# PSUM banks as tiles of their own in a fused linear-attention and MLP kernel

## The chip, the cores and the metric

The kernel is one program on one core of one Trainium2 chip. The metric is the time of one execution on the device in microseconds (us), the median of three runs. Five engines work from queues of their own, each in the order in which its instructions stand: TensorE (PE; its weight loads are shown as PEld), VectorE (DVE), ScalarE (ACT), GpSimd (POOL) and SyncE (SP), which issues the transfers here. An instruction can wait for semaphores that other engines raise.

## The reference

Three stages follow each other. Attention without a softmax over scores, for 8 batches, 8 heads, 576 positions and 64 columns a head:

```
q_s = softmax(q, axis=-1);  k_s = softmax(k, axis=2)
x   = einsum(q_s, einsum(k_s, v))          # 4608 tokens x 512
h   = x @ w_in;   g = where(h > 0, h, exp(min(h, 0)) - 1)      # layer 1, 512 -> 2048
x   = g @ w_out                                                # 2048 -> 512
h   = x @ w_in2;  g = (a0 + a1 h + a2 h^2 + a3 h^3) / (1 + |b0||h| + |b1|h^2 + 1e-6)   # layer 2
out = g @ w_out2
```

## The kernel before

Each float32 operand is split into a high and a low part, and a product is made of three matmuls. Tokens are cut into 9 blocks of 512 (index j), the 2048 inner columns into 16 steps of 128 (index f).

*Layer 1* makes, for a block and a step, one PSUM bank of h with 12 matmuls of 512 columns (L913 to L915), which ScalarE reads once (relu, L1075) and VectorE once (elu, L1081). Then 12 matmuls (L952) add into the four `acc` banks. The attention of later batches and the preparation of layer 2's weights run beside it, with their own use of the same banks (L617, L744 and others).

*Layer 2* takes two steps at once: 8 groups (p) for each block, 72 in all, each with 256 inner columns for 512 tokens. h is a 2 x 2 arrangement of pieces of 256 columns and is computed by a scheme with seven products in place of eight. The pieces are A and E in one bank, Bq and C in the next. `product` (L1187) issues six matmuls of 256 columns for each of the seven:

| name | writes | then |
|---|---|---|
| m1 | A | u1: ScalarE copies A to Bq |
| m6 | Bq (adds) | u2: ScalarE copies Bq to SBUF |
| m2, m5 | A, E | |
| m7 | Bq (adds) | u3: ScalarE copies Bq to SBUF |
| | | d1, d2: VectorE, C = E + u3's copy, E = E + u2's copy |
| m4, m3 | Bq, E (add) | h is complete |

The copies are L1196, the two adds L1203. A function of h follows, on both banks at once (128 x 1024): absb, pstart and square read h on ScalarE (L1252, L1262, L1257), pmul and pstep on VectorE (L1282, L1285), qsum on GpSimd (L1265), then root and guess on ScalarE (L1268, L1271), test, newton and pend on VectorE (L1274, L1278, L1289), and the split into high (`hi`, L325) and low part (L328, GpSimd). Eight output steps of three matmuls of 512 columns (L1362) add the result into the `acc` banks; at a block's end ScalarE copies those out and SP stores them. Layer 2's prepared weights come from DRAM in two ring loads for each group (1024 and 768 KB).

The order of the work is made by a planner (`Plan`): it runs a list of operations against assumed durations and records, for each engine, the order; the tile layer is told to keep it and adds the semaphore waits. The order is thus fixed before any wait is known. On ScalarE one group's turn in the steady state reads absb, pstart (of group n-1), u1 (of group n), square (n-1), u2 (n), hi (n-2), u3 (n), root, guess (n-1); on TensorE m1, two or three output steps, m6, m2, perhaps an output step, m5, m7, three output steps, m4, m3, two output steps, with a few variants.

PSUM has eight banks. Four are `acc`. The other four are one tile of four banks, from which `bank` hands out slices by turns:

```
banks = ps_p.tile([P, 4 * TB], F32, tag="ps", name="ps", bufs=1)
...
return warmed(banks[:, i * TB:(i + n) * TB])
```

So layer 1's tiles go round four slices, and layer 2's group n has the slices 0 and 1 or 2 and 3, by turns. Which instruction waits for which is worked out for each tile from the accesses to it.

Of the kernel before, what the change touches and what calls it, by code (L numbers as in the profile page):

```python
# [9 lines left out]
F32 = mybir.dt.float32  # L10
# [3 lines left out]
AF = mybir.ActivationFunctionType  # L14
ALU = mybir.AluOpType
AX = mybir.AxisListType
PSUM = bass.MemoryType.PSUM
DRAM = bass.MemoryType.DRAM

P = 128  # L20
TB = 512
# [173 lines left out]
def linear_attention_elu_rational(  # L195
# [31 lines left out]
    nc = tc.nc  # L227
# [7 lines left out]

    main = ctx.enter_context(tc.tile_pool(name="main", bufs=1))
    acc_p = ctx.enter_context(tc.tile_pool(name="acc_p", bufs=4, space=PSUM))
    ps_p = ctx.enter_context(tc.tile_pool(name="ps_p", bufs=1, space=PSUM))
    dram = ctx.enter_context(tc.tile_pool(name="dram", bufs=1, space=DRAM))
    attn_ctx = ExitStack()  # L240
    at = attn_ctx.enter_context(tc.tile_pool(name="at", bufs=1))
# [21 lines left out]
    op = plan.op  # L263
# [30 lines left out]
    def warmed(ps):  # L294
        for _ in range(plan.spare):
            nc.tensor.matmul(ps[:, 0:P], ident, ident, start=True, stop=True)
        plan.spare = 0
        return ps

    banks = ps_p.tile([P, 4 * TB], F32, tag="ps", name="ps", bufs=1)  # L300
    n_banks = [0]

    def bank(n=1):
        i = n_banks[0] % 4
        n_banks[0] += n
        assert i + n <= 4
        return warmed(banks[:, i * TB:(i + n) * TB])

    def acc_bank():
        return warmed(acc_p.tile([P, TB], F32, tag="acc", name="acc"))  # L310
# [1 line left out]
    def two(ap):  # L312
        return ap.rearrange("p (h c) -> p c h", h=2)
# [191 lines left out]
    pair = {}  # L505
# [645 lines left out]
    def plan_group(j, p):  # L1151
        s = step_of(1, j, 2 * p) - (EARLIER[p] if j == 0 and p < len(EARLIER) else 0)
        b = {}
        w, ((we, wek), (wl, wlk)) = plan_ring(j, p)
        x = xf[j]
# [18 lines left out]
        def u(n):  # L1174
            return b["u"][:, n * HT:(n + 1) * HT]

        def product(region, part, k, form, start):
            def fn(e):
                if k == 0 and part == 0:
                    b["h"] = bank(2)  # L1180
                o = turned(region())
                n = 0
                for i in range(2):
                    for wl_, xl in ((0, 0), (0, 1), (1, 0)):
                        lhsT = w[part][:, k, wl_ * HT + i * P:wl_ * HT + (i + 1) * P]
                        rhs = x["t", form][:, i, xl * HT:(xl + 1) * HT]
                        nc.tensor.matmul(o, lhsT, two(rhs), start=start and n == 0, stop=n == 5, skip_group_check=True)  # L1187
                        n += 1
            return fn

        def copy(dst, src):
            def fn(e):
                if "u" not in b and dst is not Bq:
                    b["u"] = f32_tile(ukind[0], ukind[1], *(ukind[2] if len(ukind) > 2 else []))
                if e == "ACT":
                    nc.scalar.activation(out=dst(), in_=src(), func=AF.Copy)  # L1196
                else:
                    nc.vector.tensor_scalar(out=dst(), in0=src(), scalar1=1.0, scalar2=None, op0=ALU.mult)
            return fn

        def add(dst, ps, n):
            def fn(e):
                nc.vector.tensor_tensor(out=dst(), in0=ps(), in1=u(n), op=ALU.add)  # L1203
            return fn

        def put(name, engines, fn, after, **kw):
# [144 lines left out]
        else:  # L1351
            o = chain(slice(0, 2 * TB), True, keep)
# [14 lines left out]
        for n, (i, q) in enumerate(order):  # L1367
            rank = s + AT["out"] * 2 / PERIOD + n * 0.25
            o = op(PE(0.66), out_mm(i, q), [ready[q], slot_ready[1, 2 * p + q, 1]], rank, follow=[last.get("mm_out")],
                   take=["acc"] if p == 0 and q == 0 else [], free=[(gkind, keep["g"])] if n == 7 else [])  # L1370
# [30 lines left out]
    for n in range(2 * KF):  # L1401
        f, which = divmod(n, 2)
# [10 lines left out]
    for p in range(KF // 2):  # L1413
# [5 lines left out]
        o = op(SP, load, [stored["wo", 2 * p], stored["wo", 2 * p + 1]], step_of(0, NB - 1, 2 * p) + 4.0, take=[f"w{p}_1"], extra=4.5)  # L1419
# [11 lines left out]
    with tc.manual_schedule():  # L1431
# [26 lines left out]
        o = op(SP, load_ab, [in_ops[0, 1, 0]], 0.0)  # L1458
        op(ACT(0.2), minus_a, [o, in_ops[0, 2, 0]], 0.0)
        o = op(ACT(0.2), abs_b1, [o, in_ops[0, 2, 0]], 0.0)  # L1460
# [72 lines left out]
```

## Time and profile before

| | |
|---|---|
| median of 3 runs | 2142.43 us (2139.59 to 2142.44) |
| profiled execution | 2129.99 us, its span 2128.2 us |
| busy in the span | TensorE 1710.3 us (80%), VectorE 1088.3 (51%), ScalarE 1084.9 (51%), GpSimd 686.6 (32%) |
| mean granted TensorE clock | 0.951 |
| DMA | 307.47 MB, 144 GB/s |

The span runs from the first to the last instruction. The granted clock is a share of TensorE's full clock: 1.00 is 2.4 GHz, 0.5 is 1.2 GHz. Layer 2's first product starts at 964.3 us, its last at 2106.6 us. "Idle before, and its releaser" is the time in which an engine stood still before an instruction, and the instruction that ended last among those it waited for.

### The profile page before, as it was taken

Reading aid. Unit: us, or ns where it says so; the run is one execution under the profiler, and the core shown is the slowest. Engines: PE = TensorE matmul, PEld = TensorE weight load, DVE = VectorE, ACT = ScalarE, POOL = GpSimd, SP = SyncE. Lnnn points to the kernel's source line nnn. Section 1 sums busy time; section 2 is a strip of 40 time slices with the busy share of each in tenths; the row PEclk is TensorE's granted clock in tenths of the full one; section 3 lists DMA queues with packets and bytes.
Section 4 is the critical chain, followed back from the end, with each engine's and each line's share of the span. In section 5 each row is a group of like instructions: output and inputs, shape, how many; then the busy total and the mean of one; then the engine's idle time right before and its main releaser. Section 6 shows DMA issues by size and latency. Waiting matters only on the chain.

```text
span 2128.2 us, 25372 instructions
## 1 busy us (share of the span) xinstructions
PE 1710.3 (80%) x9626; PEld 1409.1 (66%) x9626; DVE 1088.3 (51%) x1518; ACT 1084.9 (51%) x1689; POOL 686.6 (32%) x457
## 2 busy tenths in 40 slices
PE   8798878898888898988777777787877777777777
PEld 6576667677677677766656566666656666666666
DVE  7587665656475655212444444444444444444445
ACT  6566554556464554334555545454554545445444
POOL 3002543434353433222353332323333232323322
PEclk9999999999999999999899989999998989999989
DMA  8413542433342421153565444443534444443441
GB/s 311 165 47 117 186 164 89 162 122 127 112 157 92 171 90 75 60 191 131 174 222 180 142 154 154 166 166 143 173 124 158 168 173 145 167 152 107 162 148 35
DMA packets 83338, 307.47 MB, mean 144 GB/s; under 512 B 8720, under 2 KB 8720, under 8 KB 70928
## 3 DMA queue, kind: packets, MB, share of 16 engines
q1 hardware_dynamic: 83216, 305.85, 41.1%
q8 instruction: 76, 1.25, 0.2%
q14 instruction: 46, 0.38, 0.1%
HBM read 238.18 MB, written 67.63 MB: 144 GB/s over the span
## 4 chain that ended last, share of the span: by engine, by line
PE 54%; ACT 20%; DVE 17%; issue 4%; DMA 3%; POOL 1%; SPq 0%; DVEq 0%; ACTq 0%; POOLq 0%
PE ps L1187 20%; PE acc L1362 8%; PE acc L952 8%; PE ps L913 6%; PE ps L915 5%; PE ps L914 5%; DVE p L1285 4%; DVE p L1282 4%; ACT p L1262 4%; ACT s L1257 4%; DVE m L1081 3%; DMA x<-fo 2%; ACT m L1075 2%; ACT m L1196 2%; ACT a L1252 1%
## 5 line engine op out<-in xcount | busy, mean ns | idle before, releaser
L1187 PE MATMUL ps<-xf,ring 128*128 128x256 f32 x3024 | 459.2, 302 | 272.4 <-DVE p L1282 88.8
L1187 PEld LDWEIGHTS ps<-xf,ring 128*128 128x128 f32 x3024 | 404.2, 207 | 368.2 <-DVE p L1282 104.0
L1362 PE MATMUL acc<-w_out,g 128*128 128x512 f32 x1728 | 443.9, 400 | 0.8 <-ACT g L325 0.8
L952 PE MATMUL acc<-gs,w_out 128*128 128x512 f32 x1728 | 411.5, 384 | 7.2 <-DVE gs L328 2.5
L952 PEld LDWEIGHTS acc<-gs,w_out 128*128 128x128 f32 x1728 | 326.8, 191 | 62.2 <-ACT gs L325 4.4
L1265 POOL TENSOR_TENSOR s<-s,a 128x1024 f32<-128x1024 f32 x72 | 168.8, 2345 | 588.2 <-ACT s L1257 577.4
L1362 PEld LDWEIGHTS acc<-w_out,g 128*128 128x128 f32 x1728 | 329.0, 203 | 40.6 <-ACT g L325 1.2
L913 PE MATMUL ps<-xs,w_in 128*128 128x512 f32 x576 | 236.3, 410 | 108.3 <-ACT m L1075 45.9
L1196 ACT ACTIVATE m<-ps 128x256 f32<-128x256 f32 x142 | 54.5, 384 | 357.8 <-PE ps L1187 291.0
L914 PE MATMUL ps<-xs,w_in 128*128 128x512 f32 x576 | 223.8, 389 | 0.0
L328 POOL TENSOR_TENSOR g<-p,g 128x1024 fp32r<-128x1024 f32 (+1 forms) x71 | 167.3, 2356 | 174.4 <-ACT g L325 163.5
L915 PE MATMUL ps<-xs,w_in 128*128 128x512 f32 x576 | 223.4, 388 | 0.0
L913 PEld LDWEIGHTS ps<-xs,w_in 128*128 128x128 f32 x576 | 111.6, 194 | 166.3 <-DVE m L1081 64.4
L1081 DVE SCALAR_TENSOR_TENSOR m<-m,ps 128x512 f32<-128x512 f32 x144 | 98.7, 686 | 237.7 <-PE ps L915 122.9
L1282 DVE TENSOR_TENSOR p<-p,ps 128x1024 f32<-128x1024 f32 (+1 forms) x73 | 88.1, 1206 | 227.8 <-ACT s L1257 111.7
L1075 ACT ACTIVATE m<-ps 128x512 f32<-128x512 f32 x144 | 85.8, 596 | 215.2 <-PE ps L915 130.8
L328 POOL TENSOR_TENSOR gs<-m,gs 128x512 fp32r<-128x512 f32 x85 | 110.0, 1295 | 228.0 <-ACT gs L325 221.5
L1285 DVE SCALAR_TENSOR_TENSOR p<-p,a_sb,ps 128x1024 f32<-128x1024 f32 (+1 forms) x73 | 92.4, 1266 | 142.3 <-PE ps L1187 69.5
L1274 DVE SCALAR_TENSOR_TENSOR s<-s,a 128x1024 f32<-128x1024 f32 (+1 forms) x73 | 89.1, 1222 | 92.2 <-ACT a L1271 90.6
L1203 DVE TENSOR_TENSOR ps<-ps,m 128x256 f32<-128x256 f32 x142 | 61.4, 432 | 145.9 <-ACT m L1196 135.8
L325 ACT ACTIVATE gs<-m 128x512 fp32r<-128x512 f32 x144 | 89.9, 625 | 87.1 <-DVE m L1081 42.7
L1252 ACT ACTIVATE a<-ps,b_sb 128x1024 f32<-128x1024 f32 (+1 forms) x73 | 80.4, 1103 | 87.9 <-PE ps L1187 65.7
(152 smaller groups left out, 2146.8 us busy)
## 6 DMA issues: line engine op xcount, KB each, us to landing
ring<-wf SPq DMA_DIRECT2D x72, 1024.0 KB, 5.2
ring<-wf SPq DMA_DIRECT2D x72, 768.0 KB, 4.6
x<-fo SPq DMA_DIRECT2D x54, 512.0 KB, 2.9
xf<-x SPq DMA_DIRECT2D x47, 512.0 KB, 6.0
wf<-fo SPq DMA_DIRECT2D x24, 512.0 KB, 2.8
out_dram<-e SPq DMA_DIRECT2D x36, 256.0 KB, 2.2
bits<-in_moe_w_in_dram SPq DMA_DIRECT2D x8, 1024.0 KB, 11.2
bits<-in_moe_w_out_dram SPq DMA_DIRECT2D x8, 1024.0 KB, 12.0
```

What stands on the lines that cost most here:

```text
L328: engine[e].tensor_tensor(out=lo, in0=src, in1=hi.bitcast(F32), op=ALU.subtract)
L913: nc.tensor.matmul(o, w[:, 0, kk, :], two(x[:, 0]), start=(kk == 0), stop=False)
L914: nc.tensor.matmul(o, w[:, 0, kk, :], two(x[:, 1]), start=False, stop=False)
L915: nc.tensor.matmul(o, w[:, 1, kk, :], two(x[:, 0]), start=False, stop=(kk == KD - 1))
L952: nc.tensor.matmul(turned(o), lhsT, two(rhs), start=(f == f0 and n == 0), stop=(f == f1 and n == 2))
L1075: nc.scalar.activation(out=b["m"], in_=b["h"], func=AF.Relu, scale=-1.0)
L1081: nc.vector.scalar_tensor_tensor(out=b["m"], in0=b["m"], scalar=-1.0, in1=b["h"], op0=ALU.add, op1=ALU.max)
L1187: nc.tensor.matmul(o, lhsT, two(rhs), start=start and n == 0, stop=n == 5, skip_group_check=True)
L1265: engine[e].tensor_tensor(out=b["s"][:, c], in0=b["s"][:, c], in1=b["a"][:, c], op=ALU.add)
L1282: nc.vector.tensor_tensor(out=b["p"][:, c], in0=b["p"][:, c], in1=h(), op=ALU.mult)
L1285: nc.vector.scalar_tensor_tensor(out=b["p"][:, c], in0=b["p"][:, c], scalar=a_sb[:, 1:2], in1=h(), op0=ALU.add, op1=ALU.mult)
L1362: nc.tensor.matmul(turned(o), b["g"][:, gl, c], two(wo[:, wl_]), start=p == 0 and q == 0 and n == 0, stop=p == KF // 2 - 1 and q == 1 and ...
```

## The change

The four banks are no longer one tile. Two pools, one at either side of PSUM, have two one-bank tiles each in layer 1. When layer 2 starts to use a pool's place, the pool is closed and opened again with one tile of two banks, so that group n and group n+1 write different tiles. Inside such a pair, the products, copies and adds of a group are recorded, with the bank that each touches (A and E are bank 0, Bq and C bank 1), and any two on different engines that share no bank are declared to need no order. The reads of h by the function that follows are not recorded.

```diff
-    ps_p = ctx.enter_context(tc.tile_pool(name="ps_p", bufs=1, space=PSUM))
+    ps_ctx = [ExitStack(), ExitStack()]
+    ps_p = [c.enter_context(tc.tile_pool(name=f"ps_{i}", bufs=2, space=PSUM, side=("left", "right")[i])) for i, c in enumerate(ps_ctx)]
...
-    banks = ps_p.tile([P, 4 * TB], F32, tag="ps", name="ps", bufs=1)
+    def bank():
+        i = n_banks[0] // 2 % 2
+        n_banks[0] += 1
+        return warmed(ps_p[i].tile([P, TB], F32, tag="ps", name="ps", bufs=2))
...
-    def bank(n=1):
-        i = n_banks[0] % 4
-        n_banks[0] += n
-        assert i + n <= 4
-        return warmed(banks[:, i * TB:(i + n) * TB])
+    paired = [False, False]
+
+    def bank_pair():
+        assert n_banks[0] % 2 == 0
+        i = n_banks[0] // 2 % 2
+        n_banks[0] += 2
+        if not paired[i]:
+            paired[i] = True
+            ps_ctx[i].close()
+            ps_p[i] = ctx.enter_context(tc.tile_pool(name=f"pair_{i}", bufs=1, space=PSUM, side=("left", "right")[i]))
+        return ps_p[i].tile([P, 2 * TB], F32, tag="pair", name="pair", bufs=1)
...
+        def apart(ins, e, *regions):
+            ins = ins.ins
+            for other, e2, r2 in b["seen"]:
+                if e2 != e and not set(r2) & set(regions):
+                    tc.declare_no_dep(ins, other, reason="other bank")
+            b["seen"].append((ins, e, regions))
+
+        where = {A: 0, E: 0, Bq: 1, C: 1}
...
-                    b["h"] = bank(2)
+                    b["h"], b["seen"] = bank_pair(), []
...
-                        nc.tensor.matmul(o, lhsT, two(rhs), start=start and n == 0, stop=n == 5, skip_group_check=True)
+                        apart(nc.tensor.matmul(o, lhsT, two(rhs), start=start and n == 0, stop=n == 5, skip_group_check=True),
+                              "PE", where[region])
...
-                if e == "ACT":
-                    nc.scalar.activation(out=dst(), in_=src(), func=AF.Copy)
-                else:
-                    nc.vector.tensor_scalar(out=dst(), in0=src(), scalar1=1.0, scalar2=None, op0=ALU.mult)
+                apart(nc.scalar.activation(out=dst(), in_=src(), func=AF.Copy), e, *(where[x] for x in (dst, src) if x in where))
...
-                nc.vector.tensor_tensor(out=dst(), in0=ps(), in1=u(n), op=ALU.add)
+                apart(nc.vector.tensor_tensor(out=dst(), in0=ps(), in1=u(n), op=ALU.add), e, where[dst], where[ps])
```

On every engine the instructions stand in the same order as before; what changes is what they wait for. (Line numbers shift by 10 in layer 1 and by 17 to 19 in layer 2; the pairs are called `pair`.) The first place is TensorE's queue in the middle of layer 2: m1, two output steps, m6, m2, an output step, m5 of one group. Before:

```order
L1187 MATMUL ps<-xf,ring 128x256 [waits DMAHW4_49,Activation_49]
L1187 MATMUL ps<-xf,ring 128x256 x5
L1362 MATMUL acc<-w_out,g 128x512 x2
L1362 MATMUL acc<-w_out,g 128x512 [waits Pool_49]
L1362 MATMUL acc<-w_out,g 128x512 x3
L1187 MATMUL ps<-xf,ring 128x256 [waits Activation_49]
L1187 MATMUL ps<-xf,ring 128x256 x5
L1187 MATMUL ps<-xf,ring 128x256 [waits DMAHW5_49,DVE_49]
L1187 MATMUL ps<-xf,ring 128x256 x5
L1362 MATMUL acc<-w_out,g 128x512 x3
L1187 MATMUL ps<-xf,ring 128x256 [waits DVE_49]
L1187 MATMUL ps<-xf,ring 128x256 x5
```

And now, with m7 as the last:

```order
L1206 MATMUL pair<-xf,ring 128x256 [waits DMAHW2_49,PE_49]
L1206 MATMUL pair<-xf,ring 128x256 x5
L1379 MATMUL acc<-w_out,g 128x512 x2
L1379 MATMUL acc<-w_out,g 128x512 [waits Pool_49]
L1379 MATMUL acc<-w_out,g 128x512 x3
L1206 MATMUL pair<-xf,ring 128x256 [waits Activation_49]
L1206 MATMUL pair<-xf,ring 128x256 x11
L1379 MATMUL acc<-w_out,g 128x512 x3
L1206 MATMUL pair<-xf,ring 128x256 x6
L1206 MATMUL pair<-xf,ring 128x256 [waits DMAHW3_49,Activation_49]
L1206 MATMUL pair<-xf,ring 128x256 x5
```

m1 waited for ScalarE, m2 and m5 for VectorE; now m1 waits for TensorE itself (the pair's last owner), m2 for nothing there (it is the second half of the row "x11"), m5 for nothing (the row "x6"). m6 names ScalarE in both, and m7 names it only now: the count it waits for has changed, to that of the copies u1 and u2 of its own group.

The second place is VectorE's queue in the same group: pmul, pstep, the two adds, test. Before:

```order
L1282 TENSOR_TENSOR p<-p,ps 128x1024 [waits PE_49,Activation_49]
L1285 SCALAR_TENSOR_TENSOR p<-p,a_sb,ps 128x1024 [waits Activation_49]
L1203 TENSOR_TENSOR ps<-ps,m 128x256 [waits Activation_49]
L1203 TENSOR_TENSOR ps<-ps,m 128x256 [waits DVE_49]
L1274 SCALAR_TENSOR_TENSOR s<-s,a 128x1024 [waits Activation_49,Pool_49]
```

And now:

```order
L1299 TENSOR_TENSOR p<-p,pair 128x1024 [waits PE_49,Activation_49]
L1302 SCALAR_TENSOR_TENSOR p<-p,a_sb,pair 128x1024 [waits DVE_49]
L1220 TENSOR_TENSOR pair<-pair,m 128x256 [waits Activation_49]
L1220 TENSOR_TENSOR pair<-pair,m 128x256 [waits DVE_49]
L1291 SCALAR_TENSOR_TENSOR s<-s,a 128x1024 [waits Activation_49,Pool_49]
```

pstep waited for a copy on ScalarE (u2 of the next group); now only for pmul ahead of it.

## Rows read from the trace of the kernel before

**Rows 1.** Stretches: from:to, length, busy us of each engine, PEclk, DMA share, GB/s

```profile
0.00:100.00 100.00, 76.80 (x511) 56.50 (x511) 63.42 (x109) 58.98 (x96) 23.46 (x22) 0.95 0.65 253
800.00:900.00 100.00, 90.41 (x409) 73.03 (x407) 38.56 (x66) 41.16 (x77) 30.72 (x28) 1.00 0.18 62
100.00:964.00 864.00, 753.45 (x4220) 615.15 (x4219) 499.22 (x890) 441.51 (x870) 304.28 (x270) 0.98 0.35 121
1004.00:2107.00 1103.00, 831.43 (x4669) 698.42 (x4668) 502.62 (x493) 555.08 (x681) 345.02 (x156) 0.92 0.45 155
```

**Rows 2.** TensorE's waits, 1004 to 2107 us: releaser, total us, times, longest

```profile
PE ps L1187 <- DVE p L1282: 88.8, 52, 2.8
PE ps L1187 <- DVE p L1285: 62.2, 50, 2.7
PE ps L1187 <- ACT s L1257: 51.1, 36, 2.2
PE ps L1187 <- ACT m L1196: 23.5, 25, 1.9
...
PE ps L1187 <- DVE ps L1203: 7.5, 7, 3.6
```

**Rows 3.** Timeline, 1311 to 1327 us: start, length, engine, what [idle before, releaser]

```profile
1311.19 0.94 PE L1187 MATMUL ps<-xf,ring 128*128 128x256 f32 x6
...
1312.16 1.21 ACT L1262 ACTIVATE p<-ps,a_sb 128x1024 f32<-128x1024 f32 x1 [1.03 <-PE ps L1187]
1313.41 0.37 ACT L1196 ACTIVATE ps<-ps 128x256 f32<-128x256 f32 x1
1313.81 1.11 ACT L1257 ACTIVATE s<-ps,b_sb 128x1024 f32<-128x1024 f32 x1
...
1314.97 1.60 PE L1187 MATMUL ps<-xf,ring 128*128 128x256 f32 x12 [0.91 <-ACT s L1257]
...
1316.69 1.22 DVE L1282 TENSOR_TENSOR p<-p,ps 128x1024 f32<-128x1024 f32 x1 [3.32 <-PE ps L1187]
1317.94 0.38 ACT L1196 ACTIVATE m<-ps 128x256 f32<-128x256 f32 x1 [3.02 <-DVE p L1282]
1318.22 1.05 ACT L325 ACTIVATE g<-p 128x1024 fp32r<-128x1024 f32 x1
...
1318.38 1.60 PE L1187 MATMUL ps<-xf,ring 128*128 128x256 f32 x12 [1.80 <-ACT m L1196]
...
1321.70 1.14 ACT L1268 ACTIVATE a<-s,qbias 128x1024 f32<-128x1024 f32 x1
1321.83 0.90 DVE L1203 TENSOR_TENSOR ps<-ps,m 128x256 f32<-128x256 f32 x2 [0.45 <-ACT m L1196]
...
1322.88 1.58 PE L1187 MATMUL ps<-xf,ring 128*128 128x256 f32 x12 [0.95 <-ACT a L1268]
...
1324.29 1.46 PE L1362 MATMUL acc<-w_out,g 128*128 128x512 f32 x6
1324.49 1.11 ACT L1252 ACTIVATE a<-ps,b_sb 128x1024 f32<-128x1024 f32 x1 [0.57 <-PE ps L1187]
...
1325.66 0.94 PE L1187 MATMUL ps<-xf,ring 128*128 128x256 f32 x6
```

**Rows 4.** Timeline of TensorE, a piece without waits, 1510 to 1515 us

```profile
1510.57 1.50 PE L1187 MATMUL ps<-xf,ring 128*128 128x256 f32 x12
1511.91 1.46 PE L1362 MATMUL acc<-w_out,g 128*128 128x512 f32 x6
1513.28 0.94 PE L1187 MATMUL ps<-xf,ring 128*128 128x256 f32 x6
```

**Rows 5.** TensorE's waits, 100 to 1004 us

```profile
PE ps L913 <- ACT m L1075: 43.1, 32, 4.9
PE ps L913 <- DVE m L1081: 42.0, 44, 2.8
```

**Rows 6.** DMA issues, 1004 to 2107 us: count, KB, median us to landing

```profile
ring<-wf SPq DMA_DIRECT2D x69, 1024.0 KB, 5.2
```

## The prediction

> **What bounds the kernel now.** I read the stretches first, then TensorE's waits, then one group of layer 2 in order of time. Layer 2 is the stretch from 1004 to 2107 us, 1103 us of the span's 2128, and TensorE is busy in only 831 of them; layer 1 between 100 and 964 us has it busy in 753 of 864 [rows 1]. The other engines have room in layer 2: ScalarE 555, VectorE 503, GpSimd 345 us of 1103, DMA 0.45 of its time. TensorE's waits there are almost all on one line, the products of a group (L1187), and they name readers of the PSUM tile `ps`: pmul (L1282) 88.8 us, pstep (L1285) 62.2, square (L1257) 51.1 [rows 2]. These readers belong to the group before. In the code a product of group n needs none of them: group n writes the other two banks of `ps`, and what it does need is a copy (L1196) or an add (L1203) of its own group, and those are named for 23.5 and 7.5 us only.
>
> The timeline of one group shows how [rows 3]. m1 issues at 1311.19; its copy u1 is done by 1313.8; but m6 starts only at 1314.97, when square of group n-1 has ended (1313.81 + 1.11 = 1314.92). The copy u2 stands ready from the end of m6 and m2 (1316.57) and starts at 1317.94, when pmul of group n-1 ends (1316.69 + 1.22 = 1317.91); the products that follow wait with it, 1.80 us. m4 and m3 wait 0.95 us. That group takes 14.47 us from m1 to m1 (1311.19 to 1325.66), of which TensorE stands still for 0.91 + 1.80 + 0.95 = 3.7 us. So the chain goes round through all three engines: a product, a read on ScalarE, a read on VectorE, a product, each behind the last, for the sole reason that all four banks are one tile.
>
> A second loss follows from the first: the granted clock is 0.92 over layer 2, against 1.00 in the stretch 800 to 900 us, where TensorE is busy 90 of 100 us [rows 1]. With the two levels 1.2 and 2.4 GHz, a mean of 0.92 is 16% of the time at the lower, 176 us.
>
> **The change, part by part.** It removes and adds no engine work worth naming and moves nothing: the instructions stand in the same order on every engine, and only what they wait for differs. Layer 2 has 72 groups (9 blocks of 8), each with 42 product matmuls, 3024 in all; about 71 groups fall in the 1103 us, so 15.5 us each.
>
> *Layer 2, the two pairs.* With the rows for TensorE: m1 no longer waits for a read, m2 and m5 no longer wait for VectorE. What a group then costs TensorE comes from a stretch where it does not wait [rows 4]: two products take 1511.91 - 1510.57 = 1.34 us, so 0.67 each, and two output steps 1513.28 - 1511.91 = 1.37, so 0.685 each. A group has 7 products and 8 output steps: 4.69 + 5.48 = 10.17 us.
>
> Do the others keep up with 10.17? I lay the group out with the durations of rows 3, m1 at 0: two output steps to 2.04, m6 2.04, m2 2.71, one output step 3.38, m5 4.07, m7 4.74, three output steps 5.41, m4 7.46, m3 8.13, two output steps from 8.80 to 10.17. A product issued in 0.67 is done 0.27 later (0.94 for the single one). So m3 of the group before is done at 9.07 - 10.17 = -1.10. ScalarE: absb to 0.01, pstart to 1.22, u1 to 1.60; m6 is due at 2.04, slack 0.44. Square to 2.71; u2 waits for m6 (done 2.98) and ends at 3.36; m7 is due at 4.74. Then hi to 4.41, u3 from 5.68 to 6.06, the two adds on VectorE to 6.96; m4 is due at 7.46, slack 0.5. Root and guess, like in length, end near 8.4; absb is due at 9.07. ScalarE needs 555/71 = 7.8 us a group, VectorE 7.1, GpSimd 4.9: all under 10.17. The floor holds, with slacks of about half a microsecond in an order that is fixed on each engine. That gives 71 x 10.17 = 722 us, and I leave the waits on the own group's copies and adds standing, 23.5 + 7.5 = 31: 753. From the other side, taking off only the three readers' waits (202 us), leaving every other wait, and giving back the half-rate time (176 us x 0.75 busy / 2 = 66): 1103 - 202 - 66 = 835. I take 775, nearer the first, because the laid-out group shows no wait that must remain: **328 us less**.
>
> *The declared independence inside a pair.* This is what frees u2 from m2, and m4 from the second add; it is in the layout above. Alone it would be worth little, since a group's own copies and adds are named in 31 us. What stays tied: absb, pstart, square, pmul and pstep read a whole pair, so each still waits for m3 and m4, and pmul still for square.
>
> *Layer 1, single banks.* The matmuls into `ps` wait 43.1 us for relu (L1075) and 42.0 us for elu (L1081) [rows 5]. Before, the next tile's matmul waits for the reader of the tile before it; after, for the reader of the bank's last owner, four banks back. Bounds: nothing to 85. But here VectorE is busy 499 of 864 us and ScalarE 442, in stretches with attention and weight work between, so a later wait will take the place of some; I take two thirds, 57. The clock is 0.98 there, 35 us at the lower level, worth at most 15 (35 x 0.87 busy / 2); I take 10. **67 us less.**
>
> *The start, 0 to 100 us*, is bound by loads (DMA 0.65 busy, 253 GB/s); 23 us are idle, I take 5, between 0 and 15.
>
> *New waits.* The new tiles add waits of TensorE on itself (a bank's last owner); the owner is four banks or two groups back, so they are over. The loads come in faster: 155 GB/s x 1103/775 = 221 GB/s, where the start ran 253. A ring load lands 5.2 us after its issue [rows 6], and its buffer is free for most of two groups, about 20 us at the new pace: hidden. Where it queues behind a block's output stores on SP's queue, that cover shrinks to a few us, at 8 changes of block.
>
> Sum: 328 + 67 + 5 = 400. The profiled execution took 2129.99 us, so 1730; the median of the runs, 2142.43, stands 12 us higher, so **1742 us**. All at their best ends: 381 + 100 + 15, 1646. All at the worst: 268 + 25 + 0, 1849.
>
> **Rivals.**
> 1. *ScalarE becomes the bound.* Its order is absb, pstart, u1, square, u2, hi, u3, root, guess, and every stall of it is passed to the next product. If its 7.8 us get 0.7 us of waiting at each of its five waits on others, a group takes 11.3 to 11.5: 71 x 11.5 + 31 = 848, 73 us over my 775: 1815. For it: slacks of 0.4 to 0.5 us. Against it: 2.4 us of free time on it in each group.
> 2. *The clock stays at its mean.* TensorE keeps being granted the lower level now and then even with the waits gone. Then 66 + 10 are not got back: 1818. Against it: 1.00 from 800 to 900 us, with TensorE busy 90%, in a stretch that also goes round the banks of `ps`. The Trainium skill's page "TensorE: Matmul & The Clock Gate", section "A second HAM failure mode: psum-queue depth-cycling", says that a kernel which takes another PSUM bank in each iteration idles briefly between its groups often enough that the clock swings. By that rule the swing would outlive the change, and the time would be this rival's; by the trace, the swing goes with the waits.
> 3. *Loads come late at the changes of block.* Two ring loads late by their full 5.2 us at each of 8 changes: 83 us, 1825. For it: SP's queue is in order, and out stores stand ahead of ring loads. Against it: none of TensorE's waits names a load now.
> 4. *Slower than before.* Products that now run while ScalarE and VectorE read other banks of the PSUM are slowed by them, which the old waits made impossible inside `ps`. Place: 42 matmuls a group at 0.112 us. To lose all 400 us they would need 400/3024 = 0.13 us more each, 0.24: from there on the kernel is slower, and at 0.27 it takes 1742 + 3024 x 0.16 = 2226. Against it: output steps (L1362) already run beside such reads, and the two from 1324.29 take as long beside absb (1.37 to m1 at 1325.66) as the two in rows 4.
> 5. *The change doesn't do what it says*: some other dependency ties the tiles as before, 2142. Against it: the waits in the new order are gone.
>
> **Numbers.** Forecast 0.68, rivals 1 to 5: 0.12, 0.10, 0.06, 0.02, 0.02. The first four are faster, 0.96; within 0.2% (4 us, about what a measurement of this kernel can tell from no change) 0.02; slower 0.02. The range 1650 to 1850 takes in both ends of the unknown terms and rivals 1 to 3.
>
> **What would show it.** Right: in layer 2 the products no longer name pmul, pstep or square as releasers; m1 to m1 near 10.2 to 10.9 us; TensorE over 90% busy and a granted clock of 0.98 or more; waits that remain name the group's own copy or add. In layer 1 the matmuls into `ps` wait for relu under 20 us. Wrong: a group time over 11.5 us with ScalarE named (rival 1), a clock still near 0.92 with few waits (rival 2), loads named as releasers (rival 3), products longer than 0.3 us at the full clock (rival 4).

## The result: 1587.66 us, and the profile after

The changed kernel takes 1587.66 us (median of 4 runs, 1587.23 to 1590.91) against 2142.43 before: a ratio of 0.741, 95% interval 0.740 to 0.743. The prediction, 1742 with a range of 1650 to 1850, had the direction and missed the size: 555 us were gained where it said 400. Its profiled execution took 1590.91 us (span 1589.1), the one before 2129.99, so the traces account for 539 of the 555:

| stage, us | before | after | gain | forecast |
|---|---|---|---|---|
| start and layer 1, to layer 1's last h matmul | 1004.6 | 851.5 | 153 | 72 |
| layer 2, from there to its last product | 1101.9 | 716.0 | 386 | 328 |
| what follows | 21.6 | 21.6 | 0 | 0 |

Both stages gave more than forecast. The stretches of the changed kernel, as in [rows 1]:

```profile
0.00:100.00 100.00, 93.88 (x624) 75.62 (x625) 88.70 (x133) 75.94 (x116) 24.18 (x22) 1.00 0.65 253
100.00:852.00 752.00, 734.91 (x4269) 623.94 (x4268) 479.87 (x877) 442.50 (x876) 314.83 (x277) 0.99 0.42 147
852.00:1568.00 716.00, 700.17 (x4664) 650.70 (x4663) 506.07 (x493) 537.70 (x682) 351.28 (x157) 1.00 0.67 239
```

TensorE is busy in 98% of layer 2 (700 of 716) and the granted clock there is 1.00. The last number says that DMA now runs at 239 GB/s, where 155 sufficed. All waits of TensorE that are left in layer 2, against [rows 2], and then, of those from 100 to 852 us, the largest and the three that are left on `ps`, against [rows 5]:

```profile
PE pair L1206 <- DVE pair L1220: 12.3, 9, 2.8
PE pair L1206 <- ACT m L1215: 2.5, 3, 1.3
PE pair L1206 <- ACT pair L1215: 0.9, 2, 0.5
```

```profile
PE acc L962 <- ACT gs L335: 5.8, 4, 2.1
...
PE ps L923 <- DVE m L1091: 2.2, 4, 1.1
PE ps L627 <- DVE m L1091: 0.3, 1, 0.3
PE ps L754 <- DVE m L1091: 0.3, 1, 0.3
```

No product names pmul, pstep or square, no matmul of layer 1 names relu, and the wait of the h matmuls on elu is down from 42.0 to 2.2 us. In layer 2, 14 waits of 15.7 us stand where there were 216 of 271.6 (a wait in which TensorE stands idle is called a stop below). One group in order of time, to be laid beside [rows 3]:

```profile
1243.22 1.11 ACT L1269 ACTIVATE a<-pair,b_sb 128x1024 f32<-128x1024 f32 x1 [0.76 <-PE pair L1206]
...
1244.31 0.83 PE L1206 MATMUL pair<-xf,ring 128*128 128x256 f32 x6
1244.98 1.46 PE L1379 MATMUL acc<-w_out,g 128*128 128x512 f32 x6
...
1245.62 1.10 ACT L1274 ACTIVATE s<-pair,b_sb 128x1024 f32<-128x1024 f32 x1
1246.28 1.50 PE L1206 MATMUL pair<-xf,ring 128*128 128x256 f32 x12
1246.76 1.22 DVE L1299 TENSOR_TENSOR p<-p,pair 128x1024 f32<-128x1024 f32 x1 [0.39 <-ACT s L1274]
...
1247.21 0.38 ACT L1215 ACTIVATE m<-pair 128x256 f32<-128x256 f32 x1 [0.48 <-PE pair L1206]
...
1248.01 1.28 DVE L1302 SCALAR_TENSOR_TENSOR p<-p,a_sb,pair 128x1024 f32<-128x1024 f32 x1
1248.27 1.50 PE L1206 MATMUL pair<-xf,ring 128*128 128x256 f32 x12
...
1250.22 0.90 DVE L1220 TENSOR_TENSOR pair<-pair,m 128x256 f32<-128x256 f32 x2 [0.92 <-ACT m L1215]
...
1251.55 1.50 PE L1206 MATMUL pair<-xf,ring 128*128 128x256 f32 x12
...
1254.18 0.83 PE L1206 MATMUL pair<-xf,ring 128*128 128x256 f32 x6
```

The group takes 1254.18 - 1244.31 = 9.87 us and no row of TensorE has an idle time. m6 starts at 1246.28, while square (to 1246.72) still reads the other pair; u2 starts at 1247.21, in the middle of pmul. The adds end at 1251.12, 0.43 before m4 is due. The ring loads land a little later than in [rows 6], and no wait names one:

```profile
ring<-wf SPq DMA_DIRECT2D x69, 1024.0 KB, 5.8
```

### The profile page after: what moved, and what is told of

It reads as the page before. It is cut to its first block, busy times and chain, and to the rows that moved or that the text cites. A ratio compares the mean times of both kernels' runs of the same rounds, so it can differ in the third digit from the quotient of the medians.

```text
span 1589.1 us, 25247 instructions
## 1 busy us (share of the span) xinstructions
PE 1545.5 (97%) x9626; PEld 1363.7 (86%) x9626; DVE 1086.4 (68%) x1518; ACT 1066.5 (67%) x1689; POOL 692.8 (44%) x457
## 4 chain that ended last, share of the span: by engine, by line
PE 72%; DVE 9%; DMA 6%; ACT 6%; POOL 4%; issue 3%; SPq 0%; DVEq 0%; POOLq 0%; ACTq 0%
PE acc L1379 20%; PE pair L1206 19%; PE acc L962 17%; PE ps L923 5%; PE ps L925 5%; PE ps L924 5%; DMA x<-fo 3%; POOL fo L338 1%; DVE fo L338 1%; POOL s L1282 1%; DMA st<-in_moe_w_in_dram 1%; PE ps L754 1%; ACT fo L335 1%; PE ps L627 1%; DVE m L1091 1%
## 5 line engine op out<-in xcount | busy, mean ns | idle before, releaser
L962 PE MATMUL acc<-gs,w_out 128*128 128x512 f32 x1728 | 416.9, 387 | 15.8 <-ACT gs L335 5.8
L1379 PE MATMUL acc<-w_out,g 128*128 128x512 f32 x1728 | 414.2, 380 | 0.8 <-ACT g L335 0.8
L1206 PEld LDWEIGHTS pair<-xf,ring 128*128 128x128 f32 x3024 | 376.8, 191 | 33.7 <-DVE pair L1220 15.4
L1206 PE MATMUL pair<-xf,ring 128*128 128x256 f32 x3024 | 381.4, 275 | 15.8 <-DVE pair L1220 12.3
L962 PEld LDWEIGHTS acc<-gs,w_out 128*128 128x128 f32 x1728 | 328.1, 192 | 74.5 <-ACT gs L335 10.9
L1379 PEld LDWEIGHTS acc<-w_out,g 128*128 128x128 f32 x1728 | 308.2, 190 | 34.9 <-ACT g L335 1.2
L923 PE MATMUL ps<-xs,w_in 128*128 128x512 f32 x576 | 219.9, 382 | 2.2 <-DVE m L1091 2.2
L925 PE MATMUL ps<-xs,w_in 128*128 128x512 f32 x576 | 218.7, 380 | 0.0
L924 PE MATMUL ps<-xs,w_in 128*128 128x512 f32 x576 | 218.6, 380 | 0.0
L1299 DVE TENSOR_TENSOR p<-p,pair 128x1024 f32<-128x1024 f32 (+1 forms) x73 | 88.0, 1205 | 59.5 <-ACT s L1274 58.8
L923 PEld LDWEIGHTS ps<-xs,w_in 128*128 128x128 f32 x576 | 108.9, 189 | 21.9 <-issue 3.5
L925 PEld LDWEIGHTS ps<-xs,w_in 128*128 128x128 f32 x576 | 109.0, 189 | 15.7 <-DVE w_in L338 0.2
L924 PEld LDWEIGHTS ps<-xs,w_in 128*128 128x128 f32 x576 | 109.0, 189 | 15.3 <-DVE xs L338 0.2
L1269 ACT ACTIVATE a<-pair,b_sb 128x1024 f32<-128x1024 f32 (+1 forms) x73 | 80.3, 1102 | 52.2 <-PE pair L1206 51.7
L1215 ACT ACTIVATE m<-pair 128x256 f32<-128x256 f32 x142 | 54.4, 383 | 78.0 <-PE pair L1206 77.0
```

Of the source, the lines that this page charges most:

```text
L923: nc.tensor.matmul(o, w[:, 0, kk, :], two(x[:, 0]), start=(kk == 0), stop=False)
L924: nc.tensor.matmul(o, w[:, 0, kk, :], two(x[:, 1]), start=False, stop=False)
L925: nc.tensor.matmul(o, w[:, 1, kk, :], two(x[:, 0]), start=False, stop=(kk == KD - 1))
L962: nc.tensor.matmul(turned(o), lhsT, two(rhs), start=(f == f0 and n == 0), stop=(f == f1 and n == 2))
L1206: apart(nc.tensor.matmul(o, lhsT, two(rhs), start=start and n == 0, stop=n == 5, skip_group_check=True), "PE", where[region])
L1299: nc.vector.tensor_tensor(out=b["p"][:, c], in0=b["p"][:, c], in1=h(), op=ALU.mult)
```

## The experiments

All are edits of the changed kernel (e2 of the kernel before) and keep the order of the instructions, except e11 (fewer matmuls) and e12 and e15 (planned anew). "Layer 1" and "layer 2" are the two stages of the table; losses are against 851.5 and 716.0 us. Ties are put back with a helper that adds a dependency:

```diff
+    def tie(ins, others):
+        for other in others:
+            if other is not None:
+                tc.add_manual_dep(ins.ins, other.ins.name, INFO, reason="tied")
+        return ins
```

**e1, e2: pairs or declarations.** e1 drops the declarations and keeps the tiles; e2 keeps the four-bank tile and declares, within a group, what the change declares.

```diff
-                if e2 != e and not set(r2) & set(regions):
-                    tc.declare_no_dep(ins, other, reason="other bank")
+                pass
```

> The changed kernel without the declared independence: single banks in layer 1 and two-bank tiles in layer 2, as tiles of their own, and nothing declared inside a pair. Theory A (the ties between groups carry layer 2's gain, those inside a group little): u2 then waits for m2 as well, 0.7 us later, and m5 for u2; where an output step stands between m2 and m5 that is hidden, where none does the product stands about 0.6 us; about half of the 72 groups, so some 20 us on the changed kernel's 1588: 1610, between 1590 and 1640. Rival B (the declarations carry a good part): over 1700. Layer 1 as in the changed kernel, its last matmul into ps near 852 us.

> The kernel before, one tile of four banks, with the independence declared between the two banks of one group's products, copies and adds, and nothing else. Theory A: the products still wait for absb, square, pmul and pstep of the group before; only m4 is freed from the second add (0.43 us) in each of 72 groups, 31 us: 2110, between 2080 and 2142. Rival B: if the declarations carry the gain, under 1950.

Measured: e1 1619.43 us (ratio 0.755, 0.752 to 0.759), layer 2 34 us longer. e2 2084.61 (0.972, 0.968 to 0.977), layer 2 56 us shorter than before. Both lie in the ranges of theory A. The tiles carry the result; the declarations add 32 us to them, and alone, against a forecast of "little", 58.

**e3, e13: layer 1 tied again**, layer 2 as changed. e3 ties the main stream: each step's first matmul, relu and elu wait for the last accesses of the other two engines. e13 does so for every access to `ps`, attention's too (all its rows bear the helper's line, L237).

```diff
+                    tie(nc.tensor.matmul(... start=(kk == 0) ...), [ties.get("relu"), ties.get("elu")])
...
+            ties["relu"] = tie(nc.scalar.activation(... AF.Relu ...), [ties.get("in"), ties.get("elu")])
...
+            ties["elu"] = tie(nc.vector.scalar_tensor_tensor(...), [ties.get("in"), ties.get("relu")])
```

> The changed kernel with layer 1's main stream tied again: each tile's first matmuls wait for the last relu and elu recorded before them, and relu and elu for the last matmul and for each other. The attention's own uses of the banks stay untied. Theory A (the gain is the sum of the two layers' ties, each of which costs TensorE its listed wait and the end of the matmul before it): layer 1 goes back to nearly 1004 us, so 1588 + 130 = 1720, between 1690 and 1740. Rival C (the layers' gains depend on each other, or layer 1's came from the attention's ties): under 1650.

> The changed kernel with every use of the one-bank tiles in layer 1 tied as if they were one tile, attention's and the weights' uses too: each access by one of TensorE, ScalarE and VectorE waits for the last accesses of the other two. Layer 2 as in the changed kernel. Theory (all that layer 1 gained comes of the ties, attention's among them): 152 us lost, of which the main stream alone is 98, so 1735 us (1715 to 1755). Rival (the rest is not of the ties): 1690.

Measured: e3 1690.29 (0.788, 0.785 to 0.792), e13 1746.05 (0.816, 0.809 to 0.823). Layer 1 takes 948.8 us in e3 and 1005.2 in e13, where before had 1004.6: its gain is wholly that of the ties, 97 us by the main stream and 56 by the others. The main stream alone thus falls short of the 1004 us that I expected of e3, and the attention's ties, which I had left out there, make up the rest. The start and layer 1 of e13, one stretch, and the largest of its waits:

```profile
0.00:1005.00 1005.00, 870.97 (x4888) 703.97 (x4889) 572.83 (x1010) 519.16 (x991) 339.03 (x299) 0.97 0.38 135
```

```profile
PE ps L237 <- DVE m L237: 53.1, 54, 2.8
PE ps L237 <- ACT m L237: 49.5, 39, 5.1
```

TensorE is busy 871 us for work that takes 829 in the changed kernel (93.88 + 734.91), and stands still 134 instead of 23.

**e5: two two-bank tiles in layer 1** instead of four tiles of one bank.

```diff
-        return warmed(ps_p[i].tile([P, TB], F32, tag="ps", name="ps", bufs=2))
+        return warmed(two_banks[i][:, half * TB:(half + 1) * TB])
...
+    two_banks = [p.tile([P, 2 * TB], F32, tag="ps", name="ps", bufs=1) for p in ps_p]
```

> Layer 1 gets two fixed tiles of two banks each in place of four tiles of one bank; layer 2 is as in the changed kernel. Theory (the tie of tiles costs in layer 1 as in layer 2, by what it makes wait): of two neighbouring steps of layer 1 one still shares a tile with the step before it, so about half of what layer 1 gained (152 us from start to its last matmul) is lost: 1663 us, 1630 to 1690. Rival (two tiles are as good as four, since a reader two steps back is always over): 1588 to 1600. Rival (any tie makes the whole chain stop): near 1690, as with the whole main stream tied.

Measured: 1633.71 (0.760, 0.757 to 0.764). Layer 1 loses 38 us, a quarter of its gain, not half. The waits of its h matmuls on elu and relu, 100 to 889 us:

```profile
PE ps L925 <- DVE m L1093: 18.0, 21, 2.6
PE ps L925 <- ACT m L1087: 9.1, 7, 2.4
```

The direction held and the rule "half the ties, half the cost" did not: 28 waits are left of the 76 in [rows 5].

**e4: layer 2 tied**, every access of a pair waiting for the last accesses by the other two engines, with before's waits in layer 2 as a result; layer 1 as changed.

```diff
+                        if n == 0:
+                            tie(mm, [ties.get("A2"), ties.get("D2")])
...
+                ties["A2"] = tie(nc.scalar.activation(...), [ties.get("PE2"), ties.get("D2")])
+                ties["D2"] = tie(nc.vector.tensor_tensor(...), [ties.get("PE2"), ties.get("A2")])
```

> The changed kernel with layer 2 tied again as one tile of four banks would: each product waits for the last read or copy on ScalarE and on VectorE recorded before it, each of these for the last product and for the other engine's last, and nothing is declared. Theory A: layer 2 takes 1100 us again, a group 15.4 us, the granted clock there falls to 0.92, and the time is 1588 + 386 = 1974, between 1950 and 1990. Rival D (the place of the tiles in PSUM, not the waits, brought the gain): near 1588.

Measured: 1960.99 (0.914, 0.907 to 0.920). Layer 2 takes 1084.9 us, 369 more. Its stretch:

```profile
849.00:1933.00 1084.00, 827.15 (x4658) 694.54 (x4657) 502.06 (x492) 543.51 (x681) 345.44 (x157) 0.92 0.46 158
```

Busy time (827 against [rows 1]'s 831) and the clock (0.92) are those of before, on separate pairs of banks. So both come with the waits.

**e6, e7, e8, e9: the ties of products.** One at a time, m6 on square, m2 on pmul, m5 on pstep, each of the group before; e9 has all three (its lines are shown, the others have one tie each).

```diff
+                        if n == 0:
+                            tie(mm, [ties.get({"m6": "square", "m2": "pmul", "m5": "pstep"}.get(name))])
```

> One tie of before alone is put back: m6 of each group also waits for square of the group before it. Theory (TensorE's time is set by the loop that closes through ScalarE, laid out with the durations of the timeline): absb to square's end 3.5 us, then m6, m2, one output step, m5, m7, three output steps, m4, m3, back to absb: about 10.35 us a group against 9.87 now, so 72 x 0.48 = 35 us more, 1623 us (1600 to 1640). Rival (the time lost is the wait that the trace of before lists for square, 51 us, more or less): 1639 and more.

> One tie alone: m2 of each group also waits for pmul of the group before it. Theory (the laid-out loop): absb to pmul's end 4.76 us, from m2 back to absb 6.15, 10.91 us a group against 9.87: 72 x 1.04 = 75 us more, 1663 us (1640 to 1690). Rival (only the idle time that before lists for pmul counts, 89 us, alone): 1677. The time lost, less the idle time that the trace lists for pmul, is what each stop costs beside its listed wait.

> One tie alone: m5 of each group also waits for pstep of the group before it. Theory (the laid-out loop): absb to pstep's end 6.07 us, from m5 back to absb 4.88, 10.95 us a group against 9.87: 72 x 1.07 = 77 us more, 1665 us (1640 to 1690). Rival (only the idle time that before lists for pstep, 62 us): 1650. If the three ties' losses add up to less than the 373 us of the whole layer 2 tied, what is missing comes from their acting together (ScalarE and VectorE also waiting on each other) and from the clock, which should stay at 1.00 with one tie alone.

> The three ties of products put back together (m6 waits for square, m2 for pmul, m5 for pstep, each of the group before); readers, copies and adds wait as in the changed kernel. Alone the three cost 22, 47 and 51 us of layer 2. Theory (the 369 us of the whole of layer 2 tied come from a ring that needs both kinds of tie, products on readers and readers on products): the three loops run side by side, so that the longest sets the time: 51 us and a little, 1648 us (1635 to 1670). Rival (losses add): 121 us, 1709. Rival (the ties of the products are the whole loss): near 1950.

Measured: 1609.68, 1630.82, 1636.08 and 1646.3 us. Layer 2 loses 22, 47, 51 and 62 us. The three single losses were forecast at 35, 75 and 77, as if every group lost the same; but the tie makes TensorE wait in only 32 to 43 of the 72 groups. In e9 the loops run side by side, as expected, and do not add (121). The stretches of e7 and e9:

```profile
844.00:1607.00 763.00, 715.10 (x4660) 657.96 (x4659) 505.28 (x492) 538.52 (x681) 350.88 (x157) 0.99 0.64 224
```

```profile
847.00:1625.00 778.00, 729.21 (x4666) 655.52 (x4665) 502.64 (x493) 538.96 (x682) 350.97 (x157) 0.99 0.63 220
```

Here a stop shows its second price. In e7 TensorE waits 54 times where the changed kernel waits 14 times, and is also busy 715.1 instead of 700.2 us for the same matmuls: 14.9/40 = 0.37 us a stop, beside its listed wait. By the same count it is 0.33 in e9 (29.0/88), 0.43 in e8 (15.4/36) and 0.45 in e6 (12.1/27). Part of this is the clock: the traces' records of the granted clock have TensorE at 1.2 GHz for 10 us of layer 2 in each of these runs, and at no time there in the changed kernel. That is worth some 5 us of busy time (an estimate: half of the 9 to 10 us in which it was busy at that level). Without it a stop costs 0.26 to 0.29 us in all four.

**e10: the other half.** e4 without the two lines on products, so that readers, copies and adds stay tied, and no product waits for a reader of the group before.

```diff
-                        if n == 0:
-                            tie(mm, [ties.get("A2"), ties.get("D2")])
```

> The other half alone: in layer 2 the readers of h, the copies and the adds wait for each other and for the last product as in one tile, across groups too, and a group's own copies and adds hold its products regardless of the bank; but no product waits for a reader of the group before. Theory (the ring needs both halves): pmul waits for m2, u2 for pmul, m5 for u2: absb to u2's end 5.17 us, from m5 back to absb 4.88, 10.1 us a group, where the lack of the declarations alone gave 34 us: 20 to 60 us more, 1635 us (1610 to 1660). Rival (the loss is the rest beside the products' ties): 369 - 51 = 318, 1906.

Measured: 1720.25 (0.801, 0.798 to 0.804). Layer 2 loses 136 us; I had 20 to 60. One group of its timeline:

```profile
1262.46 1.11 ACT L1281 ACTIVATE a<-pair,b_sb 128x1024 f32<-128x1024 f32 x1 [2.63 <-DVE a L1307]
...
1265.54 1.11 ACT L1286 ACTIVATE s<-pair,b_sb 128x1024 f32<-128x1024 f32 x1 [0.58 <-PE pair L1213]
...
1266.69 1.22 DVE L1311 TENSOR_TENSOR p<-p,pair 128x1024 f32<-128x1024 f32 x1 [2.94 <-ACT s L1286]
...
1268.01 0.38 ACT L1223 ACTIVATE m<-pair 128x256 f32<-128x256 f32 x1 [1.35 <-DVE p L1311]
...
1268.44 0.94 PE L1213 MATMUL pair<-xf,ring 128*128 128x256 f32 x6 [1.62 <-ACT m L1223]
...
1269.49 1.28 DVE L1314 SCALAR_TENSOR_TENSOR p<-p,a_sb,pair 128x1024 f32<-128x1024 f32 x1 [1.58 <-PE pair L1213]
1270.81 0.38 ACT L1223 ACTIVATE m<-pair 128x256 f32<-128x256 f32 x1 [1.47 <-DVE p L1314]
...
1271.22 0.90 DVE L1230 TENSOR_TENSOR pair<-pair,m 128x256 f32<-128x256 f32 x2 [0.45 <-ACT m L1223]
...
1273.88 1.11 ACT L1281 ACTIVATE a<-pair,b_sb 128x1024 f32<-128x1024 f32 x1 [0.56 <-PE pair L1213]
```

From absb to absb it takes 11.42 us, each row following the one above (by way of u1, m6 and m2 between the first two, and of m4 and m3 ahead of the last): my layout ended at m5 and left out that pstep waits for m5 and u3 for pstep. So this half makes a ring (a closed round of waits) by itself, a shorter one. Still the parts do not make the whole: 62 (e9) + 136 (e10) = 198 of e4's 369. With both, the products too stand in the ring, and it is the 14.47 us of [rows 3].

**e14: everything tied**, on the separate banks, nothing declared.

```diff
+                if any(x.startswith(("ps", "pair")) for x in names):
+                    for who, other in ties.items():
+                        if who != self.who:
+                            tc.add_manual_dep(ins.ins, other.ins.name, INFO, reason="tied")
...
```

> The changed kernel's banks and order of work, with every wait of the one four-bank tile put back in both layers, and the independence inside a pair not declared. Theory (the waits are the whole of it): as the kernel before, 2143 us (2120 to 2160). Rival (the separate tiles bring something beside the waits, or the two layers' losses overlap): the sum of the parts tied alone, 1588 + 152 + 373 = 2113, or less.

Measured: 2119.29 (0.990, 0.986 to 0.994). Of 555 us the waits alone take back 532; layer 1 has 1005.8 us and layer 2 1097.8 (before 1004.6 and 1101.9). That is just under my 2120 to 2160 and, with the losses that e13 and e4 measured, the sum of the parts: 1588 + 158 + 373 = 2119. What the last 1% is stays open; the spans of the two traces, 2125.3 and 2128.2, differ by 3 us only.

**e11: less work for TensorE.** The third matmul (high part of g by low part of the weights) of each output step of layer 2 is left out.

```diff
-                for n, (gl, wl_) in enumerate(((0, 0), (0, 1), (1, 0))):
+                for n, (gl, wl_) in enumerate(((0, 0), (1, 0))):
```

> Leaves out the third matmul (high part of g by low part of the weights) of each of layer 2's 576 output steps, so TensorE has 576 matmuls of 512 columns less; all else as in the changed kernel. If TensorE alone sets layer 2's time, 576 x 0.215 = 124 us less: 1464. Theory (slacks of about half a microsecond, as laid out): the loop through u1, u2, u3, the adds, m3, absb and pstart back to u1 takes 8.5 us a group against the 8.15 that TensorE then needs: 72 x 1.4 = 101 us less, 1487 us (1470 to 1530). Rival (ScalarE already is as good as the bound at 9.87): 1570 and more.

Measured: 1533.00 (0.714, 0.711 to 0.717): 55 of TensorE's 124 us come out, less than my 101 and just outside the range. 49.6 us of its waits return, on the adds first (and 4.1 us on ring loads):

```profile
PE pair L1206 <- DVE pair L1220: 27.3, 30, 3.7
PE pair L1206 <- ACT pair L1215: 11.6, 39, 1.6
```

From square to square, 52 groups in which u3 stands ahead of root on ScalarE take 8.59 us in the median, the laid-out 8.5; 18 groups with root first take 9.67. One of these 18:

```profile
1258.35 1.10 ACT L1274 ACTIVATE s<-pair,b_sb 128x1024 f32<-128x1024 f32 x1
...
1259.54 2.61 POOL L1282 TENSOR_TENSOR s<-s,a 128x1024 f32<-128x1024 f32 x1 [3.49 <-ACT s L1274]
...
1261.46 0.83 PE L1206 MATMUL pair<-xf,ring 128*128 128x256 f32 x6
...
1262.18 1.15 ACT L1285 ACTIVATE a<-s,qbias 128x1024 f32<-128x1024 f32 x1 [1.19 <-POOL s L1282]
1263.24 0.36 ACT L1215 ACTIVATE m<-pair 128x256 f32<-128x256 f32 x1
...
1263.63 0.90 DVE L1220 TENSOR_TENSOR pair<-pair,m 128x256 f32<-128x256 f32 x2 [1.29 <-ACT m L1215]
...
1264.12 1.60 PE L1206 MATMUL pair<-xf,ring 128*128 128x256 f32 x12 [0.53 <-DVE pair L1220]
```

u3 is ready when m7 ends (1261.46 + 0.83 = 1262.29) and stands behind root, which GpSimd held until 1262.15. So TensorE is the bound of the changed kernel, and the next one is close: 8.6 us against 9.87.

**e12, e15: a better version?** The wait that is left, 12.3 us on the second add, was the target. e12 gives two of a block's four copies of `acc` to VectorE; e15 puts root behind the next group's u3.

```diff
+            e = DVE(0.62) if L == 1 and i % 2 == 0 else ACT(0.4 if shared else 0.62)
+            l = o1 = op(e, copy, [o], r, take=["e"], free=[] if shared else free)
...
```

```diff
+        if last.get("root"):
+            behind(last["root"], u3)
...
```

> The changed kernel with two of the four copies of acc to SBUF at the end of each of layer 2's blocks on VectorE in place of ScalarE. Theory: the one wait of TensorE that is left in layer 2 beside the start of a block (on the second add, 12.3 us, 9 times) comes of ScalarE's four copies (0.6 us each) ahead of u3, so up to 12 us less: 1580 us (1575 to 1590). Rival: the copies then stand ahead of the adds on VectorE, and the same wait stays: 1585 to 1600.

> The changed kernel with root of group n-1 always behind u3 of group n on ScalarE (one constraint given to the planner, which also moves a few instructions around the changes of block). In the changed kernel 18 groups have root first and take 10.52 us in the median, 52 have u3 first and take 9.87. Theory (that order is what the remaining wait on the second add, 12.3 us, comes from): 18 x 0.65 = 12 us at most, 1579 us (1575 to 1586). Rival (the order stands so where a block changes, and the copies and loads there cost it whatever the order): 1586 to 1600, no gain.

Measured: 1598.11 (0.744, 0.742 to 0.747) and 1598.78 (0.746, 0.743 to 0.749), both some 10 us slower than the changed kernel, in the rivals' ranges. In e12 the wait is about the same; in e15 part of it has moved to the copy u1. First e12, then e15:

```profile
PE pair L1210 <- DVE pair L1224: 13.0, 8, 2.4
```

```profile
PE pair L1206 <- ACT pair L1215: 8.4, 3, 4.4
PE pair L1206 <- DVE pair L1220: 7.2, 8, 4.1
```

The expectations put the waits of the changed kernel at the changes of block. Its trace shows them elsewhere for the greater part of the kernel: of the 12.3 us, 5.8 fall between 877 and 936 us, in layer 2's first block, and 6.5 behind the last two changes of block (1434 to 1536 us); between these two stretches there is none. So neither edit had 12 us to win at every change. TensorE's idle time in layer 2 stays at 16 and 17 us (16 in the changed kernel), and it is busy 7 and 5 us longer, with a granted clock of 0.99 where the changed kernel has 1.00. In both the stretch behind the last product is longer too (27.5 and 26.0 us, 21.6 in the changed kernel). No version here beats the changed kernel with the whole computation.

## Why the prediction was right in direction and wrong in size

*The mechanism was right.* Readers of the group before held the products for the tile's sake alone. e14 shows that the waits are (nearly) all of it, and e9, e10 and e4 that they make a ring through three engines: halves of it cost 62 and 136 us, the whole 369. The signs came as listed, but for the time of a group, 9.87 us where 10.2 to 10.9 was named.

*Where the 154 us are.* Three terms were mis-sized between 1742 and 1587.66: layer 1 with the start by 81 us (153 against 72), layer 2 by 58 (386 against 328), and the step from the profiled execution to the median by 15 (taken as 12 up, it came out 3 down). The best end of the sum, 1646, was too high mostly for layer 1: it was allowed 100 us with the clock and gave about 136.

*The failed step in layer 2: "I take 775, nearer the first".* The prediction had two ways to layer 2's time, the floor of 71 x 10.17 = 722 and the sum of listed waits taken off, 835, and set its value between them. The first came out, 716 measured, with some luck: two small errors offset each other. A group takes 9.87, because three output steps go out in 1251.55 - 1249.60 = 1.95 us, 0.65 each, where [rows 4] gave 0.685; 71 x 9.87 = 701, 21 less than the floor. And 15 us of waits are left that the floor did not have. [Rows 4] was not quite a piece without waits: at 1513.28 m1 starts late, behind absb of the group before, as it does in [rows 3]. Its weight load shows that, while the row of m1 lists no idle time because the matmul ahead is shown as still running:

```profile
1325.66 0.74 PEld L1187 LDWEIGHTS ps<-xf,ring 128*128 128x128 f32 x6 [0.31 <-ACT a L1252]
```

The second way missed 835 - 716 = 119 us, in two parts:
- The waits left standing. [Rows 2]'s three readers have 202 of 271.6 us; I let the other 70 stand, of which 54 went too. 21 of the 70 name absb and pstart (L1252, L1262), two more readers of the group before. A wait that is listed for a group's own copy was late because the copy itself was late in the ring.
- The price of a stop beside its wait. Busy time fell by 830 - 700 = 130 us. The clock's part of that was forecast at 66; by the trace's clock records TensorE was at 1.2 GHz for 167 us of layer 2 and busy in 145 of them, which makes 73 (an estimate: half, since products go out 213 ns apart there and 112 ns apart otherwise). The other 57 over 202 stops less are 0.28 us each, the price that e6 to e9 show. The rows show two pieces of it. Twelve products behind a stop are 1.60 us long ([rows 3], 1314.97), and 1.50 without one (1246.28 above): 0.10 us goes at the first of them. And the last matmul ahead of a stop is shown as 0.275 us where the next would have gone out after 0.112: its end, 0.16 us, has nothing to cover it. Together they are 0.26 us.

The Trainium skill, "Perfetto Trace Analysis", section "Tensor Engine Instruction (MATMUL, LD_WEIGHTS)", says that the end of a matmul is computed by the profiler and not observed. No run here shows the true end, so how a stop's time divides into idle and busy is open; the sum of both is measured by the length of the stretch. The list of waits thus told too little of the whole (272 us listed, 386 gained), and too much of one tie alone (before lists 51, 89 and 62 us for the three readers; e6 to e8 lose 22, 47 and 51).

The 31 us of copies and adds that I added to the floor as well were the same error: the layout itself showed no such wait.

*The failed step in layer 1, the larger one: "two thirds, 57", and "nothing to 85".* It gave 153 with the start, where I had 72. The bound of 85 counted two releasers of one line. e3 shows 97 for the main stream alone (78 us of listed waits and the stops), e13 another 56 from the uses by attention and weights, whose waits I had not listed. The price of a stop was left out here too. My reason for the haircut, that a later wait takes the place, did not come true: with the start, TensorE's idle time fell from 142 us to 23.

*The start:* TensorE's idle time in the first 100 us fell from 23 to 6, a gain of 17 where I took 5 and bounded it by 15. DMA moves the same 253 GB/s there before and after, so the loads, which the prediction had as the bound, were not all that held it.

*The declarations* were said to be worth little alone. They are 58 us alone (e2) and 32 on top of the tiles (e1).

*The rivals.* ScalarE as the bound (1) did not come: the forecast slacks of 0.4 to 0.5 us were there (u1 done 0.58 before m6, the adds 0.43 before m4) and sufficed; e11 shows a loop through ScalarE at 8.6 us, 1.3 below TensorE's 9.87. The clock (2) went to 1.00 with the waits, though groups still go from one pair of banks to the other 72 times. The rule of the Trainium skill that the prediction weighed there ("TensorE: Matmul & The Clock Gate", "A second HAM failure mode: psum-queue depth-cycling") did not come true as the prediction read it: with the same alternation of banks the clock is 1.00 without the waits and 0.92 with them (e4). What went with the waits is idling between groups, which the section names beside the alternation. Loads (3): DMA runs at 239 GB/s, near the 221 forecast, and no wait names a load. Slower products (4): the 3024 products have a median of 275 ns in both traces. The starts tell more, since the profile models the ends of matmuls: in the changed kernel 1566 products have ScalarE or VectorE reading other banks of the pairs all the way to the next product's start, 1047 have no such read at all, and both kinds go out 112 ns apart in the median. In the kernel before, no product ran wholly beside such a read.

## What to carry to other kernels

When an engine's idle time comes from waits that no data asks for, lay out one period with the durations of the trace. Where every slack came out positive, the busiest engine's time was the forecast to take (722 us, 716 measured), without waits that the layout does not show. Where a loop through several engines was the bound, the same kind of layout missed (35, 75 and 77 us against 22, 47 and 51 in e6 to e8, 20 to 60 against 136 in e10, 101 against 55 in e11). The list of waits does not do instead: it leaves out the price of each stop and the clock, and does not show how ties act together. Ask of every tile that holds several banks who must wait for whom: in this kernel one tile of four banks cost a quarter of the time with the same work in the same order. Ties that are cheap one by one (22, 47, 51 us) can be dear together (369), so undoing one of them tells little about all.

## What the runs showed of the hardware

- A stop of TensorE cost 0.26 to 0.29 us beside the idle time that the list of waits gives it, the clock's part taken off (before, e4, e6 to e10; in e10 31 us over 121 stops). Behind a stop the second product starts 213 ns after the first, where products otherwise go out 112 ns apart.
- The granted clock over layer 2 was 0.92 with 212 waits of 256 us in 1084 (e4), and still 0.99 with 135 waits of 109 us in 852 (e10).
- Products lost nothing to ScalarE and VectorE reading other banks of PSUM at the same time: they go out 112 ns apart beside such reads (1566 of them) and without (1047).
